# The last tile's four strided stores: issued by SyncE and ScalarE instead of SyncE and GpSimd

## The chip, the cores and the metric

The kernel runs on one core of a Trainium2 chip. A core has five engines with an instruction stream each: TensorE (PE, with its weight loads as PEld), VectorE (DVE), ScalarE (ACT), GpSimd (POOL) and SyncE (SP). Transfers between the core's memory and the chip's large memory are issued by an instruction on one of these streams and then run by themselves on 16 DMA engines; a semaphore tells when a transfer has landed. The metric is the device time of one execution, in microseconds, as the median of several runs.

## The reference

A sorting attention is followed by a Fourier mixing block. Four batches of 768 tokens with 8 heads of 64 go through the attention; its result, seen as 768 x 512 per batch, goes through a two-dimensional Fourier transform, a normalisation and a two-layer network:

```python
X = np.fft.fft(x, axis=1)
X = np.fft.fft(X, axis=2)
mixed = np.real(X).astype(np.float32)
u = x + mixed
mu = np.mean(u, axis=-1, keepdims=True)
var = np.mean((u - mu) ** 2, axis=-1, keepdims=True)
un = (u - mu) / np.sqrt(var + 1e-06)
ch = np.maximum(un @ w_ch1, 0.0) @ w_ch2
return (u + ch).astype(np.float32)
```

`x` is the attention's output; `w_ch1` is 512 x 2048 and `w_ch2` 2048 x 512. The output has 4 x 768 x 512 values of 32 bits.

## The kernel before

The host program builds one list of *steps* for all four batches. A step has a name, the engines that it may run on with a cost for each, a function that writes the instructions, the tiles that it reads and writes, and, for a DMA, the time of its transfer (`work`) and of its latency (`hop`). A planner (`Plan`, L187 to L379) keeps an estimate of when each engine is free (`free`), when the DMA queue of each issuing engine is free (`dma`) and when the eight semaphore lanes of each issuing engine are free (`lanes`). `run` (L334) takes, again and again, the step that could start earliest; `emit` (L269) writes it and moves the estimates. The planner's output is the order of the instructions on each engine. It is made on the host and costs no device time. Semaphore waits between the instructions are put in when the program is built, from what each one reads and writes.

The end of the program is the network of batch 3, second half (`mlp`, L1108). For 128 tokens at a time PE adds up 16 matmuls into one bank (L1150), VectorE adds the residual and writes a tile `outt` of 128 x 512 values (L1158), and `store` (L1163) sends it to `out`. In the Fourier part the tokens lie in another order than in the output. So 23 of the 24 tiles are written by an indirect DMA on GpSimd (L1173), which takes the row numbers from a table. The last tile, batch 3 tile 5, holds four groups of tokens that lie at a fixed stride in the output (32, 24, 24 and 48 rows), and `store` writes it with four direct DMAs at L1169. Before the change SyncE issues three of these and GpSimd the second one, of 24 rows. Every store into `out` waits for the indirect stores into `out` ahead of it, since the program cannot know that their rows differ.

After the last instruction all engines meet: SyncE waits for the semaphores of the transfers, each engine drains what it has under way (an instruction DRAIN), the engines exchange semaphores, and GpSimd clears them. The profile gives all of this the line L1393, where the host program leaves the kernel.

Of the kernel before, what the change touches and what calls it, by code (L numbers as in the profile page):

```python
# [17 lines left out]
S = 768  # L18
# [3 lines left out]
G = 6  # L22
# [102 lines left out]
class Buf:  # L125
    __slots__ = ("tag", "t", "left", "free_at")

    def __init__(self, tag):
        self.tag, self.t, self.left, self.free_at = tag, None, 0, 0.0
# [57 lines left out]
class Plan:  # L187
# [15 lines left out]
    def __init__(self, engines):  # L203
        self.engines, self.rings = engines, {}
        self.wrote, self.read = {}, {}
        self.todo = []
        self.free = dict.fromkeys(engines, 0.0)
        self.dma = {"S": 0.0, "G": 0.0}
        self.lanes = {"S": [0.0] * 8, "G": [0.0] * 8}
        self.pool = (0.0, 0.0)  # L210
        self.under_way = []
        self.began = self.half = False
# [6 lines left out]
    def step(self, name, b, on, fn, r=(), w=(), work=0, hop=0, lanes=1, bulk=False, need=None, prio=None,  # L219
             rel=0.0):  # L220
        s = Step()
        s.name, s.b, s.on, s.fn, s.work, s.hop, s.rel = name, b, on, fn, work, hop, rel
        s.lanes, s.bulk, s.port = lanes, bulk, name in self.PORT
        s.data, s.pre, s.succ, s.fin, s.by, s.extra = set(), set(), set(), None, None, []
        for key in r:
            if key in self.wrote:
                s.data.add(self.wrote[key])
        s.pre |= s.data
        for key in w:
            if key in self.wrote:  # L230
                s.pre.add(self.wrote[key])
            s.pre.update(self.read.get(key, ()))
        for key in r:
            self.read.setdefault(key, set()).add(s)
        for key in w:
            self.wrote[key] = s
            self.read[key] = set()
        s.pre.discard(s)
        s.use = list(dict.fromkeys(
            k if isinstance(k, Buf) else k[0] for k in list(r) + list(w)  # L240
            if isinstance(k, Buf) or isinstance(k, tuple) and isinstance(k[0], Buf)))
        for u in s.use:
            u.left += 1
        s.prio = need - 90e3 if need is not None else prio
        self.todo.append(s)
        return s
# [70 lines left out]
    def start(self, free, dma, lanes, landed):  # L317
        for s in self.wrote.values():
            if s in self.todo:
                continue  # L320
            s.fin = free["T"]
            if landed.get(s.name):
                s.fin = max(s.fin, landed[s.name].pop(0))
        self.half = False
        self.free = dict(free)
        self.dma = dict.fromkeys("SG", dma)
        self.lanes = lanes
        for r in self.rings.values():
            if isinstance(r, Ring):
                for h in r.held:  # L330
                    if h is not None:
                        h.free_at = free["T"]
# [50 lines left out]
def kernel(  # L383
# [27 lines left out]
    plan = Plan({"T": nc.tensor, "V": nc.vector, "A": nc.scalar, "G": nc.gpsimd, "S": nc.sync})  # L411
    step, Buf = plan.step, plan.buf
# [695 lines left out]
    def mlp(b, gr):  # L1108
# [32 lines left out]
        for t in range(3):  # L1141
            pC = Buf("bank")
            for f4 in range(4):
                if f4 == 0 and t < 2:
                    load_u(t + 1)

                def f(e, t=t, f4=f4, pC=pC):
                    ps = bank(pC, [128, DM])
                    for fc in range(4 * f4, 4 * f4 + 4):
                        nc.tensor.matmul(ps, hr[f4].t[:, fc % 4, 128 * t:128 * (t + 1)],  # L1150
                                         w2sb[:, fc, :], start=(fc == 0), stop=(fc == 15))
                pc = ("pc", b, {"T": 870}, f, [(hr[f4], j) for j in range(4)] + [("w2", f4)], [pC, "mlp"])
                if f4 < 3:
                    plan.chain(pc, prio=MLP)
                    continue
                o = Buf("outt")
                plan.chain(pc, prio=MLP)
                step("outt", b, {"V": 687}, lambda e, t=t, pC=pC, o=o: nc.vector.scalar_tensor_tensor(  # L1158
                    o.t, ur[t].t, RSC, bank(pC, [128, DM]), op0=ALU.mult, op1=ALU.add),
                    [pC, ur[t]], [o], prio=MLP - 1e8)  # L1160
                store(b, 3 * gr + t, o, MLP - 1e8)

    def store(b, q_, o, prio):  # L1163
        if (b, q_) == (B - 1, 5):
            for y, (r, n, k0, st) in enumerate((
                    (0, 32, 2 * BLK + 33, 2), (32, 24, 3 * BLK, 4),
                    (56, 24, 3 * BLK + 2, 4), (80, 48, 3 * BLK + 1, 2))):
                e_ = "G" if y == 1 else "S"
                step("store", b, {e_: 400}, lambda e, r=r, n=n, k0=k0, st=st: plan.engines[e].dma_start(  # L1169
                    out[b, k0:k0 + st * (n - 1) + 1:st], o.t[r:r + n]), r=[o], work=300, hop=1300, prio=prio)  # L1170
            return
        c = 6 * b + q_
        step("store", b, {"G": 1050}, lambda e: nc.gpsimd.indirect_dma_start(  # L1173
            out=out.rearrange("b s m -> (b s) m"),
            out_offset=bass.IndirectOffsetOnAxis(ap=idx[:, c:c + 1], axis=0),
            in_=o.t, in_offset=None), r=[o, "idx"], work=800, hop=1400, prio=prio)
# [87 lines left out]
    for half in range(2):  # L1264
        make_kron(0, half, pcol)
    step("pca", 0, {"A": 390}, lambda e: nc.scalar.activation(pca, pcol(), AF.Copy, scale=XSC / BLK),
         r=[pC, (kron[0], 1)], w=["pca"])
# [62 lines left out]
    for b in range(B):  # L1330
# [10 lines left out]
        for h in range(H):  # L1341
            n = H * b + h
# [55 lines left out]
```

## Time and profile before

| what | value |
|---|---|
| median of 3 runs | 316.94 us |
| the three runs | 312.82, 316.96, 316.94 us |
| span of the profiled execution, first to last instruction | 312.2 us |
| time of the profiled execution itself | not listed; the runs above lie 0.6 to 4.8 us over its span |
| granted TensorE clock, mean | 0.985 |
| busy: PE, DVE, ACT, POOL | 287.7, 218.6, 206.3, 137.8 us |
| DMA issued by SyncE's queue (hardware_dynamic) | 39560 packets, 28.68 MB |
| DMA issued by GpSimd's queue (software_dynamic) | 14800 packets, 16.57 MB |

The profile shows one execution. Times within it count from its first instruction. An engine's name with a q behind it (SPq, POOLq) stands for the engine's instruction sequencer: semaphore instructions, drains and the issuing of DMAs, which count as no busy time of the engine. A row of the timeline gives start, duration, engine, line, operation, and what is written from what; in square brackets stands the idle time ahead of it and what ended it. A row of the view of one line gives the operation, how many there are, their shortest, median and longest duration in ns, and the start of the first and of the last.

### The profile page before, as it was taken

How to read it: one execution, taken by the hardware profiler on the slowest of the kernel's cores; microseconds unless marked ns; L12 is line 12 of the kernel's file. 1: busy time of each engine (PE TensorE's matmuls, PEld its weight loads, DVE VectorE, ACT ScalarE, POOL GpSimd, SP SyncE). 2: the span in 40 equal slices, each digit the busy share in tenths (PEclk: the TensorE clock that was granted, in tenths of full speed). 3: DMA queues.
4: the chain of work that ended last, by engine and by line, in shares of the span. 5: the costliest groups of instructions: out<-in, count | busy, mean ns of one | idle time of the engine just before them, and what ended most of it. 6: DMA issues, size and time to landing. Idle time of an engine off the chain costs nothing.

```text
span 312.2 us, 7389 instructions
## 1 busy us (share of the span) xinstructions
PE 287.7 (92%) x2715; PEld 181.9 (58%) x2715; DVE 218.6 (70%) x489; ACT 206.3 (66%) x486; POOL 137.8 (44%) x206
## 2 busy tenths in 40 slices
PE   8879599999999798999998999999999999999990
PEld 5657577866765454555654767646556755645540
DVE  6779779998997888787579999997466764010010
ACT  6587587999884567998676759887715754704500
POOL 8634166957125899446444115462021763112020
PEclk9999979999999999999999999999999999999996
DMA  7975886999699776996997444569334337314021
GB/s 214 172 189 92 172 208 96 171 207 219 129 141 213 194 229 111 144 243 171 180 225 132 104 119 96 147 188 212 75 92 135 104 100 215 80 67 136 0 101 35
DMA packets 54396, 45.72 MB, mean 146 GB/s; under 512 B 23393, under 2 KB 46144, under 8 KB 54360
## 3 DMA queue, kind: packets, MB, share of 16 engines
q1 hardware_dynamic: 39560, 28.68, 36.0%
q0 software_dynamic: 14800, 16.57, 30.6%
q8 instruction: 21, 0.34, 0.5%
q14 instruction: 15, 0.12, 0.2%
HBM read 35.33 MB, written 12.58 MB: 153 GB/s over the span
## 4 chain that ended last, share of the span: by engine, by line
PE 59%; DVE 15%; ACT 8%; DMA 5%; issue 5%; POOL 4%; SPq 1%; POOLq 0%; DVEq 0%; ACTq 0%
PE bank L1129 21%; PE bank L1150 21%; DVE kz L484 3%; PE bank L913 3%; DMA v<-in_v_dram 2%; DMA eT<-es 2%; ACT kz L480 2%; PE bank L868 2%; POOL u L1032 1%; POOL u L1033 1%; PE bank L982 1%; PE bank L821 1%; DVE xr L875 1%; ACT un L1075 1%; SPq L690 1%
## 5 line engine op out<-in xcount | busy, mean ns | idle before, releaser
L1129 PE MATMUL bank<-unT,w1sb 128*128 128x384 f16 x512 | 90.8, 326 | 1.3 <-ACT hr L1135 1.3
L1150 PE MATMUL bank<-w2sb,hr 128*128 128x512 f16 x384 | 90.5, 379 | 0.6 <-DVE W L482 0.6
L1135 ACT ACTIVATE hr<-bank 128x384 f16<-128x384 f32 x128 | 60.4, 495 | 28.6 <-PE bank L1129 27.6
L1129 PEld LDWEIGHTS <-w1sb 128*128 128x128 f16 x512 | 48.3, 98 | 31.8 <-issue 2.0
L1173 POOL DMA_INDIRECT out_dram<-outt,idx_sb x23 | 23.1, 1005 | 81.9 <-DVE outt L1158 61.5
L1150 PEld LDWEIGHTS <-hr 128*128 128x128 f16 x384 | 35.9, 98 | 38.3 <-issue 0.8
L1158 DVE SCALAR_TENSOR_TENSOR outt<-ur,bank 128x512 f32<-128x512 f32 x24 | 16.4, 682 | 38.8 <-PE bank L1150 38.8
L826 ACT ACTIVATE sm<-bank,mns 96x96 f32<-96x96 f32 x128 | 32.6, 354 | 4.8 <-DVE mns L831 4.6
L1050 DVE BATCH_NORM_STATS2 st<-u 96x6 f32<-96x512 f32 (+1 forms) x32 | 21.9, 683 | 4.2 <-POOL u L1033 4.0
L875 DVE TENSOR_TENSOR xr<-bank,rz 96x512 f16<-96x512 f32 x32 | 22.0, 686 | 1.1
L1032 POOL TENSOR_TENSOR u<-u,P 96x257 f32<-96x257 f32 (+1 forms) x16 | 11.9, 743 | 22.8 <-DVE P L990 10.9
L524 POOL TENSOR_TENSOR v<-v 128x384 f32<-128x384 f32 x11 | 11.1, 1013 | 18.3 <-ACT v L478 18.2
L484 DVE TENSOR_SCALAR kz<-bank 64x768 f16<-64x768 f32 x16 | 15.2, 952 | 4.9 <-ACT kz L480 3.4
L478 ACT COPY u<-bank 96x512 f32<-96x512 f32 (+1 forms) x21 | 12.1, 586 | 9.0 <-PE bank L1009 6.5
L1075 ACT ACTIVATE un<-u,nm,rstd 96x512 f16<-96x512 f32 (+1 forms) x16 | 13.0, 819 | 6.9 <-DVE nm L1064 6.9
L913 PE MATMUL bank<-cso_sb,xs 96*128 96x384 f16 x64 | 13.4, 332 | 3.9 <-ACT sm L808 2.7
L478 ACT CAST W<-bank 128x384 f16<-128x384 f32 (+1 forms) x29 | 10.6, 402 | 8.6 <-PE bank L913 6.1
L682 DVE SCALAR_TENSOR_TENSOR vo<-a,bank 128x384 f16<-128x384 f16 x32 | 15.7, 542 | 0.0
L480 ACT ACTIVATE kz<-bank 64x768 f16<-64x768 f32 x16 | 12.7, 803 | 4.3 <-DVE kz L484 3.2
L831 DVE TENSOR_REDUCE mns<-bank 96x8 f32<-96x768 f32 x16 | 14.9, 943 | 0.7 <-PE bank L821 0.7
L892 DVE TENSOR_TENSOR xs<-xr 96x512 f16<-96x512 f16 x32 | 14.6, 469 | 0.7 <-PE bank L929 0.2
L808 ACT ACTIVATE sm<-bank 96x768 f32<-96x768 f32 x16 | 12.8, 800 | 3.5 <-PE bank L803 2.8
(149 smaller groups left out, 539.9 us busy)
## 6 DMA issues: line engine op xcount, KB each, us to landing
u_dram<-u SPq DMA_DIRECT2D x32, 192.0 KB
ur<-u_dram SPq DMA_DIRECT2D x24, 256.0 KB
v<-in_v_dram SPq DMA_DIRECT2D x11, 384.0 KB
vs<-vo SPq DMA_DIRECT2D x48, 65.0 KB
k<-in_k_dram POOLq DMA_DIRECT2D x15, 192.0 KB, 4.4
q<-in_q_dram POOLq DMA_DIRECT2D x15, 192.0 KB, 5.0
w1sb<-in_moe_w_ch_dram POOLq DMA_DIRECT2D x4, 512.0 KB, 6.9
w2sb<-in_moe_w_ch_dram POOLq DMA_DIRECT2D x4, 512.0 KB, 6.0
```

Of the source, the lines that this page charges most:

```text
L478: nc.scalar.copy(dst, src)
L480: nc.scalar.activation(dst, src, AF.Copy, scale=scale)
L484: nc.vector.tensor_scalar(dst, src, scale, None, op0=ALU.mult)
L826: nc.scalar.activation(sm.t[:, i], pair(pS, BLK)[:, y, i % 4], AF.Exp, bias=mn.t[:, i:i + 1], scale=-1.0)
L875: nc.vector.tensor_tensor(xr2[b % 2][0:BLK, :, D * h:D * (h + 1)].rearrange("p (t j) d -> p t j d", t=2), ps[:, :, :, 0:D], r[:, :, :, Non ...
L913: nc.tensor.matmul(ps, xs[b, hp, 1].t[:, j, :], cso[:, j, :], start=(j == 0), stop=(j == 3))
L1050: nc.vector.bn_stats(st.t[0:n], us[b, i, m].t[0:n])
L1129: nc.tensor.matmul(ps, w1sb[:, mc, 128 * fc:128 * fc + 128], unT[b, gr].t[:, mc, :], start=(mc == 0), stop=(mc == 3))
L1135: nc.scalar.activation(dst, bank(pH, [128, 384]), AF.Relu)
L1150: nc.tensor.matmul(ps, hr[f4].t[:, fc % 4, 128 * t:128 * (t + 1)], w2sb[:, fc, :], start=(fc == 0), stop=(fc == 15))
L1158: step("outt", b, {"V": 687}, lambda e, t=t, pC=pC, o=o: nc.vector.scalar_tensor_tensor(o.t, ur[t].t, RSC, bank(pC, [128, DM]), op0=ALU.mu ...
L1173: step("store", b, {"G": 1050}, lambda e: nc.gpsimd.indirect_dma_start(out=out.rearrange("b s m -> (b s) m"), out_offset=bass.IndirectOffs ...
```

## The change

The last tile's four stores are issued by SyncE and ScalarE in turn: SyncE issues the first (32 rows) and the third (24 rows), ScalarE the second (24 rows) and the fourth (48 rows). Rows, strides and sizes stay as they are. GpSimd issues none of the four; its last DMA is the indirect store of the tile before. Since ScalarE now issues DMAs, the planner gets a queue and eight lanes for it; they start as the others do.

```diff
@@ Plan.__init__
-        self.dma = {"S": 0.0, "G": 0.0}
-        self.lanes = {"S": [0.0] * 8, "G": [0.0] * 8}
+        self.dma = dict.fromkeys("SGA", 0.0)
+        self.lanes = {e: [0.0] * 8 for e in "SGA"}
@@ Plan.start
-        self.dma = dict.fromkeys("SG", dma)
-        self.lanes = lanes
+        self.dma = dict.fromkeys("SGA", dma)
+        self.lanes = dict(lanes, A=[free["A"]] * 8)
@@ store
             for y, (r, n, k0, st) in enumerate((
                     (0, 32, 2 * BLK + 33, 2), (32, 24, 3 * BLK, 4),
                     (56, 24, 3 * BLK + 2, 4), (80, 48, 3 * BLK + 1, 2))):
-                e_ = "G" if y == 1 else "S"
-                step("store", b, {e_: 400}, lambda e, r=r, n=n, k0=k0, st=st: plan.engines[e].dma_start(
+                step("store", b, {"SA"[y % 2]: 400}, lambda e, r=r, n=n, k0=k0, st=st: plan.engines[e].dma_start(
                     out[b, k0:k0 + st * (n - 1) + 1:st], o.t[r:r + n]), r=[o], work=300, hop=1300, prio=prio)
             return
```

## The prediction, made before the result was known

> **What bounds the kernel now.** I read the page's head first, then the chain that ended last, then the timeline of the last microseconds, then the instructions that the profile puts on the closing line of the program (L1393, where all engines meet). The page says where the bulk lies:
>
> ```profile
> span 312.2 us, 7389 instructions
> PE 287.7 (92%) x2715; PEld 181.9 (58%) x2715; DVE 218.6 (70%) x489; ACT 206.3 (66%) x486; POOL 137.8 (44%) x206
> ```
>
> PE holds 92% of the span, and the change touches none of its work. What can move is only what comes after the last matmul. The chain of waits from 302 us shows it, and behind it the timeline from 303.7 us (start, duration, engine, line, operation):
>
> ```profile
> 302.17 2.73 DMA out_dram<-outt,idx_sb
> 304.90 0.02 issue
> 304.93 0.02 POOLq L1169
> 304.94 0.55 issue
> 305.50 0.62 POOLq L1393
> ```
>
> ```profile
> 303.76 0.38 PE L1150 MATMUL bank<-w2sb,hr 128*128 128x512 f16 x1
> 304.23 0.69 DVE L1158 SCALAR_TENSOR_TENSOR outt<-ur,bank 128x512 f32<-128x512 f32 x1 [2.76 <-PE bank L1150]
> 305.07 1.47 SPq L1169 DMA_DIRECT2D out_dram<-outt  x3
> 305.52 0.59 POOL L1169 DMA_DIRECT2D out_dram<-outt  x1 [2.38 <-DVE outt L1158]
> ```
>
> PE ends at 303.76 + 0.38 = 304.14 us, VectorE writes the last tile until 304.92, SP issues three stores from 305.07 to 306.54, POOL one from 305.52 to 306.11. The span ends at 312.2. So 5.7 us follow in which no engine computes. The instructions of the closing line tell what fills them (first and last start in us, durations in ns; the first two rows are the answer for the stretch 305.4 to 311.2, the others that for 308 to 313):
>
> ```profile
> L1393 SPq EVENT_SEMAPHORE  x9: 28/28/28, 307.6 to 308.5; - x9
> L1393 SPq DRAIN  x2: 7/7/7, 308.6 to 308.6; - x2
> L1393 POOLq DRAIN  x1: 5923/5923/5923, 305.5 to 305.5; - x1
> ...
> L1393 POOLq EVENT_SEMAPHORE  x4: 17/17/17, 311.5 to 312.1; - x4
> L1393 POOLq DRAIN  x3: 46/103/5923, 305.5 to 311.9; - x3
> ```
>
> This is the row that decides the case. SP waits at the close for the landings (nine semaphore instructions, the last at 308.5) and reports at 308.6. POOL starts one DRAIN at 305.5, as it issues its store, and that DRAIN takes 5.92 us, to 305.5 + 5.92 = 311.42; only at 311.5 does POOL take up the semaphores by which the engines meet. SP has then waited for 311.42 - 308.6 = 2.8 us. **The end of the span is set by POOL's drain behind its own store**; 312.2 - 311.42 = 0.78 us of meeting and clearing follow. The other two drains of POOL, at 311.6 to 311.9, take 0.10 and 0.05 us, so a drain is not long in itself. The transfers do not fill that gap either (times of the stretch, its length, then busy us of PE, PEld, DVE, ACT and POOL, clock, DMA share, GB/s):
>
> ```profile
> 307.00:308.00 1.00, 0.00 (x0) 0.00 (x0) 0.00 (x0) 0.00 (x0) 0.00 (x0) 0.50 0.38 107
> 308.00:309.00 1.00, 0.00 (x0) 0.00 (x0) 0.00 (x0) 0.00 (x0) 0.00 (x0) 0.50 0.00 0
> 309.00:312.20 3.20, 0.00 (x0) 0.00 (x0) 0.00 (x0) 0.00 (x0) 0.00 (x0) 0.50 0.00 0
> ```
>
> **The change part by part.** *Before the last tile: nothing.* The planner's new row "A" starts, like those of S and G, from the value that `start` is given and is raised only by a step that issues a DMA on A. The maximum over the rows and the charges of S and G are then the same until the last four stores. I cost the program up to 304.92 at 0.
>
> *Removed: POOL's store.* Its wait (0.02), the issue gap (0.55), the 0.59 us of the DMA and the drain behind it go. POOL's last work is then the indirect store ahead of it:
>
> ```profile
> 302.17 0.97 POOL L1173 DMA_INDIRECT out_dram<-outt,idx_sb  x1 [2.91 <-DVE outt L1158]
> ...
> L1169 POOL DMA_DIRECT2D out_dram<-outt x1: 592/592/592, 305.5 to 305.5; - x1
> DMA to landing us min/median/max: 2.1/2.1/2.1
> ```
>
> POOL's drain can start some 3 us earlier. What it waits for is not written in any row, so I bound its end by the three points that it can be counted from. From its own start, which coincides with the start of the last DMA: 302.17 + 5.92 = 308.09. From the end of that DMA's instruction: 311.42 - 306.11 = 5.31 us behind it, so 302.17 + 0.97 + 5.31 = 308.45. From its landing: the store landed at 305.52 + 2.1 = 307.6, the drain ended 3.8 us later; the indirect store lands at 302.17 + 2.73 = 304.90, so 308.70. All three lie within 0.6 us. Below them stands the drain without any tail (0.05 to 0.10 us, the other two rows): POOL would then be done at 303.2 and decide nothing. I take 308.45, the middle.
>
> One rule bears on this row. The Trainium skill, GPSIMD Engine Reference, section "Instruction dispatch", says that the first call of freshly loaded code costs about 6 us (5.95 measured there) without an instruction of its own in the profile. The 5.92 us here agree in size, though no row shows a code load; by that rule the price is fixed and is paid from the point where POOL stops, which is the first of the three points, 308.09.
>
> *Moved: the stores.* SP issues the 32-row and the second 24-row store, ACT the first 24-row and the 48-row one. ACT has no work left that this could delay:
>
> ```profile
> 293.88 0.49 ACT L1135 ACTIVATE hr<-bank 128x384 f16<-128x384 f32 x1 [0.16 <-PE bank L1129]
> ...
> L1169 SPq DMA_DIRECT2D out_dram<-outt x2: 336/364/391, 305.1 to 305.5; - x2
> ...
> L1169 SPq DMA_DIRECT2D out_dram<-outt x1: 324/324/324, 306.2 to 306.2; - x1
> ...
> SPq L1169 <- DMA out_dram<-outt,idx_sb: 6.4, 2, 3.5
> ```
>
> ACT is idle from 294.4. The added wait is the one that SP has already (last row): all indirect stores into `out` must have landed, the last at 304.90, and the tile must be written, 304.92. Both come together, and nothing but ACT's share of the closing meeting is queued behind ACT's stores, so ACT can issue from 305.07 as SP does. An issue by ACT is nowhere in this trace; the nearest rows are SP's three, 0.32 to 0.39 us, and the step from SP's first to its third store is 306.2 - 305.07 = 1.13 us, of which the 24-row store alone takes from about 305.45 to 306.2, 0.76 us. If ACT works like SP and beside it, its 48-row store starts at 305.07 + 0.76 = 305.83, 0.37 earlier than the same store on SP now, and SP reports at 308.6 - 0.37 = 308.25. If ACT needs twice SP's price, or the two queue for one another, it starts at 305.07 + 2 x 0.76 = 306.59, and SP reports at 309.0. I take 308.6, near the middle: today's time. All four stores use the same rows of the tile and the same bytes; POOL's transfer of 48 KB now starts a little earlier and may push the others by the little that is inside these bounds.
>
> **The sum.** The meeting begins at the later of POOL (308.09 to 308.70) and SP (308.25 to 309.0): I take 308.6, against 311.42 now. With the 0.78 us behind it the span ends at 309.4, bounds 309.0 to 309.8: 2.8 us less (2.4 to 3.2). The median of the runs shown, 316.94, is 4.74 us above the profiled span and the lowest, 312.82, 0.62 above; the time of the profiled execution itself is not given. I take the same 2.8 us off the median: 314.1 us (313.7 to 314.5), 0.9% less. What a measurement can tell from no change here is about 2%, and the three runs shown differ by 1.3% among themselves.
>
> **The rivals.**
>
> *The drain follows the last transfer of any queue.* Then POOL waits for more than its own stores, and a drain started earlier ends no earlier. SP's waits put the last landing at 308.4 (its last two semaphore instructions stand at 308.4 and 308.5), 3.0 us ahead of the drain's end. The 48-row store lands between 0.37 us earlier and 0.4 later, and the time is 316.6 to 317.3. Against it: DMA share is 0 from 308 on while the drain goes on. The Trainium skill, "DMA: Bandwidth & Descriptors", section "Issuing engines are not separate DMA queues", speaks in the same direction: all queues run on the same 16 engines, and spreading DMAs saves issue time alone. By that rule the change is worth the 0.37 us of issue, on an engine that is not last, and the time is 316.9. Chance 0.12.
>
> *The drain's tail grows with what POOL's last DMA moves: slower.* The indirect store now stands last, and it is larger:
>
> ```profile
> DMA packets 80, 0.26 MB, mean 219 GB/s; under 512 B 16, under 2 KB 16, under 8 KB 80
> ...
> q0 software_dynamic: 32, 0.05, 31.9%
> ```
>
> (the indirect store's packets between 303.5 and 304.7 us, and those of POOL's direct store between 306.6 and 307.3.) With packets the tail of 5.31 us becomes 5.31 x 80/32 = 13.3 us, POOL is done at 303.14 + 13.3 = 316.4, the span ends at 317.2 and the time is 321.9; counted from the landing, 3.8 x 2.5 = 9.5, it is 319.9. It costs time from the point where the tail is over 311.42 - 303.14 = 8.28 us, 1.56 times today's. For it: one long drain, behind one kind of DMA, cannot show a fixed price. Against it: the drain outlasts its transfer by 3.8 us, so bytes alone do not explain it. Chance 0.08.
>
> *ACT's own queue of DMAs costs something outside the span or at its first issue,* which no row prices: ACT issues no DMA now. It eats the gain when it comes to 2.8 us; bounded by nothing and by the 4.74 us that lie around the span at the median, it gives 314.1 to 318.8, with 316.5 in the middle. Chance 0.10.
>
> *The runs fall low.* One of three runs was 4.1 us below the other two, whatever the reason. If most of the new runs fall so, the median is 312.82 - 2.8 = 310.0. Chance 0.20.
>
> **How the numbers follow.** The forecast has the remaining 0.50. The range takes in the low runs and the rival without gain, 309.5 to 317.3; outside are the longer tail and a part of the queue's price, and a stray below, together under 0.2. Faster by over 2% means below 310.6: the low runs, 0.20. Slower by over 2% means above 323.3: only a longer tail together with a price for the queue, 0.03. The rest, 0.77, is within 2%.
>
> **What would show it.** In the changed profile POOL's long DRAIN should start at about 302.2 and end between 308.1 and 308.7; the SP semaphores of the closing line should end at 308.2 to 309.0; the two ACT stores should start near 305.1 and 305.8 and take 0.3 to 0.6 us; the last VectorE tile should still end near 304.9. I am wrong if the drain still ends near 311.4 (any queue), if it is longer than 8 us (packets), or if ACT's stores start late. A gain far from 2.4 to 3.2 us in the span would mean that the drain counts from something else.

## The result and the profile after

With the change the median of 12 runs is 311.21 us, against 314.97 us of 12 runs of the kernel before: a ratio of 0.9885 with a 95% interval of 0.9846 to 0.9924, or 3.6 us less (2.4 to 4.9). The same kernel, timed once more in a later run beside the kernel before, gave 0.9919 (0.9885 to 0.9953). It is a gain, and it is under the 2% mark. The ratio leaves out the slower runs of both kernels, of which the profiled execution of the changed kernel is one (315.81 us, its longest, granted clock 0.970), so its middle is not compared with anything here; only its close is.

The timeline of the changed kernel from 306.5 us, in the columns known from before (here and below the rows of PE and PEld are left out):

```profile
306.94 0.97 POOL L1172 DMA_INDIRECT out_dram<-outt,idx_sb  x1 [2.94 <-DVE outt L1158]
308.97 0.69 DVE L1158 SCALAR_TENSOR_TENSOR outt<-ur,bank 128x512 f32<-128x512 f32 x1 [2.76 <-PE bank L1150]
309.93 1.04 SPq L1168 DMA_DIRECT2D out_dram<-outt  x2
309.93 0.99 ACTq L1168 DMA_DIRECT2D out_dram<-outt  x2
```

And its closing line, now L1392, with the line of the four stores, L1168:

```profile
L1392 SPq EVENT_SEMAPHORE  x11: 17/28/28, 311.0 to 314.0; - x11
L1392 POOLq EVENT_SEMAPHORE  x4: 17/17/17, 313.3 to 313.9; - x4
L1392 POOLq DRAIN  x3: 46/97/6417, 306.7 to 313.8; - x3
L1392 SPq DRAIN  x3: 7/7/7, 313.2 to 313.5; - x3
...
L1168 SPq DMA_DIRECT2D out_dram<-outt x2: 333/334/336, 309.9 to 310.6; - x2
L1168 ACTq DMA_DIRECT2D out_dram<-outt x2: 349/476/603, 309.9 to 310.6; - x2
```

The last VectorE tile ends at 308.97 + 0.69 = 309.66 and the span at 314.0: 4.4 us lie between, where there were 312.2 - 304.92 = 7.3. POOL's long DRAIN now starts at 306.7, ahead of the last indirect store, and ends at 306.7 + 6.42 = 313.1. SP reports at 313.2 to 313.3 and POOL takes up the meeting at 313.3. POOL's drain and SP's waits for the landings, which were 2.8 us apart, end together. ACT's two stores are there, at 0.60 and 0.35 us. Up to the last stores each engine runs the same instructions in the same order in both traces, so the planner's new row moved nothing else.

### The profile page after: what moved, and what is told of

Its sections match the earlier page's. It is cut to its first block, busy times and chain, and to the rows that moved or that the text cites. A ratio compares the mean times of both kernels' runs of the same rounds, so it can differ in the third digit from the quotient of the medians.

```text
span 314.0 us, 7394 instructions
## 1 busy us (share of the span) xinstructions
PE 291.1 (93%) x2715; PEld 184.6 (59%) x2715; DVE 217.8 (69%) x489; ACT 206.3 (66%) x486; POOL 137.1 (44%) x205
## 4 chain that ended last, share of the span: by engine, by line
PE 57%; DMA 16%; POOL 7%; DVE 6%; ACT 5%; issue 3%; SPq 3%; POOLq 0%; DVEq 0%; ACTq 0%
PE bank L1150 22%; PE bank L1129 21%; DMA vs<-vo 5%; DMA w2sb<-in_moe_w_ch_dram 4%; DMA unT<-in_q_dram 4%; PE bank L913 2%; DMA u_dram<-u 2%; PE bank L868 2%; SPq L690 2%; DVE kz L484 1%; PE bank L821 1%; POOL u L1033 1%; POOL kz L1226 1%; POOL u L1032 1%; ACT kz L480 1%
## 5 line engine op out<-in xcount | busy, mean ns | idle before, releaser
L1150 PE MATMUL bank<-w2sb,hr 128*128 128x512 f16 x384 | 91.6, 382 | 2.2 <-DMA w2sb<-in_moe_w_ch_dram 2.2
L787 DVE TENSOR_REDUCE mxs<-bank 96x8 f16<-96x768 f32 x16 | 14.7, 946 | 0.8 <-PE bank L784 0.7
L868 PEld LDWEIGHTS <-eT 97*128 97x128 f16 (+1 forms) x256 | 11.6, 102 | 5.9 <-DMA vs<-vo 2.1
```

The costliest lines, as they stand in the source:

```text
L868: nc.tensor.matmul(ps[0:wide(i).stop - BLK * i, i // 4, i % 4], et[0:97, wide(i)], vs[2 * (b % 2) + h // 4][:, i, (D + 1) * (h % 4):(D + 1 ...
```

## The experiments

**What was to be told apart.** The theory on record: the end is set by POOL's closing drain, which counts from the end of POOL's own last DMA, and the change gains by letting POOL stop one tile earlier. Rivals: the gain is in issuing the stores from two engines; the drain follows the last transfer of any queue; the drain grows with what the last DMA moves; and, formed after the result, that the drain itself is dear and it does not matter what stands ahead of it.

All kernels are read by one table. "Tail" is the time from the end of the last VectorE tile to the end of the span, "drain" the end of POOL's closing drain and "SP" the moment at which SP reports, both counted from the end of that tile, "behind POOL" the time from the end of POOL's last instruction to the end of the drain, all in us from each kernel's trace:

| kernel | drain | behind POOL | SP | tail |
|---|---|---|---|---|
| before | 6.5 | 5.3 | 3.7 | 7.3 |
| the change | 3.5 | 5.2 | 3.6 | 4.4 |
| e11, the change again | 3.5 | 5.2 | 3.4 | 4.3 |
| e1, all four on SP | 3.6 | 5.2 | 3.9 | 4.7 |
| e2, POOL keeps its store, ACT helps | 6.5 | 5.3 | 3.5 | 7.3 |
| e4, the change and a POOL copy | 5.5 | 5.2 | 3.4 | 6.3 |
| e5, before and a middle drain | 2.9 | 1.6 | 3.5 | 4.3 |
| e6, the change and a middle drain | 0.1 | 1.9 | 3.6 | 4.4 |
| e7, three engines and a middle drain | 3.1 | 1.8 | 3.6 | 4.4 |
| e8, the change, largest first | 3.5 | 5.2 | 3.3 | 4.2 |
| e9, before and an early drain | 4.2 | 3.1 | 3.4 | 5.0 |
| e10, largest first and a middle drain | 0.2 | 1.9 | 3.4 | 4.2 |

In each row the tail is the later of the two ends plus 0.8 us, to the rounding. Of e4, e5, e8 and e9 there is one execution each, so they are read by these times within the trace and not by their total.

**e1: POOL's store away, ACT not used.**

```diff
-                step("store", b, {"SA"[y % 2]: 400}, ...
+                step("store", b, {"S": 400}, ...
```

> All four stores of the last tile are issued by SP, none by POOL and none by ACT: the change without its ACT part. Measure: from the end of the last VectorE tile to the end of the span (7.3 us before, 4.4 us with the change). Theory (POOL's closing drain counts some 5.3 us from the end of POOL's own last DMA instruction, and the change gains by ending POOL's DMAs one tile earlier): POOL's drain ends 3.5 us behind the tile as with the change, SP's landings come some 0.8 us later than with the change because of four issues in a row, so 5.0 to 5.4 us, and a ratio to before near 0.993. Rival (the gain is in issuing the stores from two engines at once): 7.3 us or more, ratio 1.00 or above. Rival (the drain follows the last transfer of any queue): the drain ends 3 us behind the last landing, 8 us.

Measured: ratio 0.9935 (0.9887 to 0.9983), tail 4.7 us. The timeline and the closing line of this kernel:

```profile
300.31 0.97 POOL L1172 DMA_INDIRECT out_dram<-outt,idx_sb  x1 [3.05 <-DMA out_dram<-outt,idx_sb]
302.23 0.69 DVE L1158 SCALAR_TENSOR_TENSOR outt<-ur,bank 128x512 f32<-128x512 f32 x1 [2.77 <-PE bank L1150]
303.21 1.84 SPq L1168 DMA_DIRECT2D out_dram<-outt  x4
...
L1392 POOLq DRAIN  x3: 46/97/6418, 300.1 to 307.3; - x3
L1392 SPq DRAIN  x3: 7/7/7, 306.8 to 307.1; - x3
```

The tile ends at 302.92, the drain at 300.1 + 6.42 = 306.5 and SP reports at 306.8. Taking the store off POOL alone brings the tail from 7.3 down to 4.7, where the whole change brings it to 4.4. The rival of two engines is wrong: without ACT nearly all of the gain is there. The rival of any queue is wrong too: here the drain ends before SP has its last landing. The tail was expected at 5.0 to 5.4 and came at 4.7: SP's four issues took 1.84 us, and SP reported only 0.3 us later than with the change.

**e2: ACT helps, POOL keeps its store.**

```diff
-                step("store", b, {"SA"[y % 2]: 400}, ...
+                step("store", b, {"SGSA"[y]: 400}, ...
```

> POOL keeps its 24-row store, ACT takes the 48-row store from SP: the ACT part of the change alone. Theory of POOL's own drain: it starts with POOL's store and ends 5.2 to 5.3 us behind that store's end as before, so 7.3 us from the last tile to the end of the span, ratio 1.00. Rival (issuing from more engines gains): 4.4 to 6.9 us, ratio 0.99 to 0.997.

Measured: ratio 1.0044 (0.999 to 1.0098), tail 7.3 us:

```profile
304.26 0.69 DVE L1158 SCALAR_TENSOR_TENSOR outt<-ur,bank 128x512 f32<-128x512 f32 x1 [2.77 <-PE bank L1150]
305.54 0.59 POOL L1168 DMA_DIRECT2D out_dram<-outt  x1 [2.38 <-DVE outt L1158]
...
L1392 POOLq DRAIN  x3: 46/103/5920, 305.5 to 311.9; - x3
L1392 SPq DRAIN  x3: 7/7/7, 308.4 to 311.7; - x3
```

SP reports at 308.4 instead of 308.6 and waits for the same drain, to 305.5 + 5.92 = 311.4. ACT's part of the change alone is worth nothing.

**e4: what does the drain count from?**

```diff
+            step("touch", b, {"G": 60}, lambda e: nc.gpsimd.tensor_copy(landed[0:1], o.t[0:1, 0:1]), r=[o], prio=prio)
             return
```

> The changed kernel with one more POOL instruction: a copy of one value of the last tile into a scratch tile, which waits for the last tile and so ends some 0.3 us behind it. It asks what POOL's closing drain counts from. If from POOL's last DMA instruction (something that the DMA leaves behind): the drain's end stays 5.2 to 5.3 us behind the end of the indirect store, and the span ends 4.4 us behind the last tile as with the change. If from the last instruction of any kind (the drain itself is dear, as with code that must be loaded first): the drain ends 5.2 to 5.3 us behind the copy, and the span ends 6.3 us behind the last tile.

```profile
303.43 0.97 POOL L1173 DMA_INDIRECT out_dram<-outt,idx_sb  x1 [2.93 <-DVE outt L1158]
305.47 0.69 DVE L1158 SCALAR_TENSOR_TENSOR outt<-ur,bank 128x512 f32<-128x512 f32 x1 [2.77 <-PE bank L1150]
306.22 0.18 POOL L1170 CAST landed<-outt 1x1 f16<-1x1 f32 x1 [1.83 <-DVE outt L1158]
...
L1393 POOLq DRAIN  x3: 46/97/5443, 306.2 to 312.2; - x3
L1393 SPq DRAIN  x3: 7/7/7, 309.5 to 311.9; - x3
```

The copy ends at 306.40 and the drain at 306.2 + 5.44 = 311.6, 5.2 us behind the copy and 7.2 us behind the DMA. The tail is 6.3 us, and SP has waited 2 us. So the theory's "behind the DMA" falls: a copy of one value brings two thirds of the loss back. The DMA had landed at 303.43 + 2.7 = 306.1, before the copy ended, so the drain did not wait for it. The 5.2 us are the drain's own, and at the close they count from the end of POOL's last instruction, whether that is a direct DMA, an indirect one or this copy. What they are spent on is not shown.

**e5: is every drain so dear?** In the kernel before, one more drain three tiles ahead of the last, in a stretch in which POOL waits:

```diff
+            if c == 20:
+                nc.gpsimd.drain()
```

> The kernel before with one more POOL DRAIN, behind the indirect store three tiles ahead of the last. If only a first drain is dear (code that must be loaded once): the new drain takes 5.9 us, the closing one under 0.7 us, SP's landings set the end, and the span ends 4.5 us behind the last tile instead of 7.3. If every drain behind a DMA takes 5.2 to 5.3 us from that DMA's end: both drains do, and it stays at 7.3 us. If drains of POOL in the middle end at the landing, the new one takes about 3 us.

The timeline, the middle drain (L1180), the closing line and POOL's store:

```profile
283.09 0.97 POOL L1175 DMA_INDIRECT out_dram<-outt,idx_sb  x1 [2.64 <-DVE outt L1158]
302.38 0.69 DVE L1158 SCALAR_TENSOR_TENSOR outt<-ur,bank 128x512 f32<-128x512 f32 x1 [2.77 <-PE bank L1150]
303.73 0.59 POOL L1169 DMA_DIRECT2D out_dram<-outt  x1 [2.37 <-DMA out_dram<-outt,idx_sb]
...
L1180 POOLq DRAIN  x1: 6624/6624/6624, 282.9 to 282.9; - x1
...
L1398 POOLq DRAIN  x3: 51/103/2255, 303.7 to 307.1; - x3
L1398 SPq DRAIN  x3: 7/7/7, 306.5 to 306.9; - x3
...
DMA to landing us min/median/max: 2.1/2.1/2.1
```

The middle drain takes 6.62 us and ends 5.4 behind its DMA, in the shadow of POOL's idle time. (e6, e7 and e10 have it too. It ends 5.25 to 5.65 us behind its DMA in the four, but in each 2.5 to 2.6 us behind the landing, which takes 3.7 to 4.1 us there and 2.7 at the close. There a later landing goes with a later end.) The closing one then takes 2.26 us: it ends at 303.7 + 2.26 = 306.0, some 0.2 us behind the landing at 303.73 + 2.1 = 305.8. The tail is 4.3 us with POOL still issuing its store: **what the change takes off the tail, one drain in an idle place takes off too.** Behind a drain that ended 14 us earlier, the closing one ends just after the landing.

**e6: the change and the middle drain** (both edits together).

> The changed kernel with a DRAIN of POOL behind the indirect store three tiles ahead of the last, where POOL is idle. If a drain that has run shortly before is cheap, POOL's closing drain ends with the landing of its last indirect store, within 0.3 us of the last VectorE tile, and not 3.5 us behind it; then SP's waits for the landings alone set the end, 4.3 to 4.4 us behind the last tile, as with the change (4.37): ratio to before as for the change, 0.985 to 0.993. If the cheap drain of the earlier run was a matter of the direct store being POOL's last, the drain stays at 3.5 us behind the tile.

```profile
304.26 0.69 DVE L1158 SCALAR_TENSOR_TENSOR outt<-ur,bank 128x512 f32<-128x512 f32 x1 [2.77 <-PE bank L1150]
...
L1397 POOLq DRAIN  x3: 46/97/3077, 302.0 to 309.1; - x3
L1397 SPq DRAIN  x3: 7/7/7, 308.5 to 308.8; - x3
```

POOL is done at 302.0 + 3.08 = 305.1, and SP at 308.5 sets the end; ratio 0.9893 (0.9849 to 0.9938). The tail stays where it was, 4.4, so behind the change nothing more is to be had from the drain alone: the landings end as late (in the change's two profiles once after the drain and once 0.1 us before it).

**e8, e7, e10: can the landings come earlier?** e8 lets SP issue 48 rows and then 24, ACT 32 and then 24:

```diff
-                    (0, 32, 2 * BLK + 33, 2), (32, 24, 3 * BLK, 4),
-                    (56, 24, 3 * BLK + 2, 4), (80, 48, 3 * BLK + 1, 2))):
+                    (80, 48, 3 * BLK + 1, 2), (0, 32, 2 * BLK + 33, 2),
+                    (32, 24, 3 * BLK, 4), (56, 24, 3 * BLK + 2, 4))):
```

> The changed kernel with its stores in another order: SP 48 rows then 24, ACT 32 rows then 24. Theory: POOL's drain ends 3.5 us behind the last tile whatever SP does, so the span ends 4.2 to 4.4 us behind it, no earlier than 0.15 us ahead of the change (4.37), even if SP's landings come 0.3 us earlier. Rival (the landings alone set the end): 4.0 to 4.1 us.

SP reports 3.3 us behind the tile, the drain ends at 3.5, the tail is 4.2 us, as the theory had it. e7 has the middle drain and this order with POOL back, `{"SAGS"[y]: 400}`:

> Mid drain on POOL, and the four stores over three engines with the largest first: SP 48 rows, then the second 24; ACT 32 rows; POOL the first 24. With the cheap drain, POOL's store costs no tail: POOL is done about 2.9 us behind the last tile, SP 3.0 to 3.4, and the span ends 3.8 to 4.2 us behind the last tile (4.37 with the change, 7.3 before): ratio 0.985 to 0.992. If the drain is dear whenever a direct store stands last, the end is at 7.3 us as before.

Its tail is 4.4 us and not 3.8 to 4.2; the ratio is 0.9955 (0.9915 to 0.9995). The cheap drain is there (3.1 us behind the tile), but the stores from three engines land no earlier, and SP reports at 3.6. e10 is e8 with the middle drain:

> The changed kernel with both the DRAIN of POOL three tiles ahead of the last and the order of e8 (SP 48 rows then 24, ACT 32 rows then 24). POOL should be done 0.2 us behind the last tile, SP 3.3 us as in e8, so the span ends 4.0 to 4.15 us behind the last tile, 0.1 to 0.2 us under e8 (4.25) and 0.3 under the change (4.37). Against the change that is 0.1%, below what the times can tell; the ratio to before should be 0.985 to 0.991. If POOL's drain plays no part in e8, it stays at 4.2 to 4.3.

Its tail is 4.2 us and not 4.0 to 4.15, with POOL done at 0.2 and SP at 3.4; ratio 0.9876 (0.9806 to 0.9946). SP reported 0.1 us later than in e8, so taking the drain away bought nothing there. With e8's it is the shortest tail measured, but 0.2 us under the change is less than the times can tell, and SP's report itself came at 3.6 and at 3.4 in two profiles of the changed kernel.

**e11: the change once more.**

> The change itself once more, beside the kernel before on the same chip as the run above, for a profile that is less disturbed in its middle. The tail from the last VectorE tile to the end of the span should be 4.3 to 4.5 us again, with POOL's drain ending 5.2 us behind the end of the indirect store, and the ratio to before 0.985 to 0.992.

Tail 4.3 us, the drain 5.2 us behind POOL, ratio 0.9919: as expected.

**e9: how long does a drain keep?** The drain of e5 behind the first indirect store instead (`c == 0`):

> The kernel before with the additional DRAIN of POOL behind its first indirect store, at about 103 us, with some 60 POOL operations of other kinds between it and the close. If only the first drain behind the start is dear, the closing one is cheap (2.3 us) and the span ends 4.3 us behind the last tile. If a drain becomes dear again when POOL has done other work in between, both take 5.2 us from the end of what stands ahead of them, and it stays at 7.3 us. The drain in the middle can also delay the work there; only the close is to be compared.

```profile
104.60 1.09 POOL L1175 DMA_INDIRECT out_dram<-outt,idx_sb  x1 [0.17 <-issue]
109.39 0.72 POOL L1032 TENSOR_TENSOR u<-u,P 96x257 f32<-96x257 f32 x1 [3.70 <-issue]
...
L1180 POOLq DRAIN  x1: 6991/6991/6991, 102.3 to 102.3; - x1
...
L1398 POOLq DRAIN  x3: 46/103/3707, 308.8 to 313.0; - x3
L1398 SPq DRAIN  x3: 7/7/7, 311.6 to 312.8; - x3
```

Neither expectation holds. The early drain ends at 102.3 + 6.99 = 109.3 and holds POOL up for 3.7 us behind its DMA (104.60 + 1.09 = 105.69 to 109.39), and the closing drain, 200 us later, ends 3.1 us behind POOL's store: less than 5.3, more than 1.6. The tail is 5.0.

**A reading that no run tests.** The price of a drain may grow with what POOL has issued since its last one. The first row is POOL's first drain of the program, in the kernel before; the others are the packets of POOL's queue in e9 up to 109.3 us and from there on (number, MB, share of the DMA engines):

```profile
L1382 POOLq DRAIN  x1: 192/192/192, 0.3 to 0.3; - x1
...
q0 software_dynamic: 9200, 8.00, 51.2%
...
q0 software_dynamic: 5600, 8.57, 18.6%
```

With no packet behind it that first drain took 0.19 us. With 160 to 192 packets since the last drain the closing one ended 1.6 to 1.9 us behind POOL's last instruction (e5, e6, e7, e10), with 5600 it was 3.1, with 9200 it was 3.6, and with 14608 to 14800 it was 5.2 to 5.65. The order fits in every trace, e4's among them, and the time since the last drain does not give it: 102 us stand before the 3.6 and 200 us before the 3.1. But no run changes the packets alone, so this is a guess to be tested and not a cause.

## Why the prediction was right, and where it was not

*That the drain sets the end, and that 2.8 us go:* right. The tail fell from 7.3 to 4.4 us, 2.9 us; e1 and e2 show that POOL's store carried it and ACT's part did not. The sum ended on SP's report, 3.7 us behind the tile, with POOL 0.15 us ahead of it; measured were 3.4 to 3.6 for SP and 3.5 for POOL. The measured 0.9885 stands beside the 0.991 that the forecast comes to (314.1 / 316.94), inside the interval.

*What the drain counts from:* the value taken, 5.31 us from the end of POOL's last DMA, came out at 5.2, so the sum was good. The other two points were off by some 0.3 us each: from the start of the DMA the drain ended 313.1 - 306.94 = 6.2 us later and not 5.92, and from the landing at 306.94 + 2.7 = 309.6 it ended 3.5 us later and not 3.8. But all three points tied the end to POOL's last DMA, and e4 shows that it need not be one: the drain was as long behind a copy, with that DMA landed. Counting from the DMA held because a DMA happened to be POOL's last instruction in both kernels, and 5.31 us from one direct DMA held for an indirect one without a row that said so. That much was luck.

*The rule weighed there,* in the Trainium skill, GPSIMD Engine Reference, section "Instruction dispatch": a first call of freshly loaded code costs about 6 us. The prediction put this at 308.09, which counts from the start of the DMA; POOL stops at its end, 303.14, and 5.92 us from there is 309.06. Measured from that end were 5.2 us. A dear drain and a cheap one soon after (e4, e5) would fit such a rule, but POOL's first drain of the program took 0.19 us, so the dear one is not the first; that code is loaded is shown by no row, and e9's 3.1 us fit neither a first call nor a later one. What makes a drain dear stays open.

*The stores:* SP was taken to report at today's 3.7 us behind the tile, and did at 3.4 to 3.6. The two engines do queue for one another: SP's second store started 0.70 us behind its first (309.93 and about 310.63), as in every kernel here in which ACT issues, where the kernel before and e1 had 0.38, and ACT's first issue took 0.60 us. The 0.76 us that the prediction gave a 24-row store are no fixed price: in e1 SP went on 0.76 us after the first of them and 0.37 us after the second. So ACT gives 0.3 to 0.5 us against four stores on SP (e1: 3.9), and no more. That is the size of the issue time, as the Trainium skill has it in "DMA: Bandwidth & Descriptors", section "Issuing engines are not separate DMA queues". That the change would be worth no more than this, as the rival took from that rule, did not hold here, because of the drain.

*The rivals:* the last transfer of any queue is refuted by e1, and by e6, where POOL is done 3.4 us before SP reports; the tail that grows with size by the change itself, 5.2 us behind 80 packets against 5.3 behind 32; a price of ACT's queue outside the span shows nowhere, the time lying 1.7 to 1.9 us over the span in every timed run, with ACT's queue or without.

*The absolute time* is the term that was mis-sized. The forecast took the median of three runs, 316.94, and put 4.74 us around the profiled span. With 1.8 us around it, that execution took some 314.0 us by estimate, and the median of 12 runs is 314.97. The predicted 314.1 is 2.9 us above the measured 311.21: about 2.0 from that median, the rest from the gain, 3.8 between the medians instead of 2.8. So 311.21 lies outside the 313.7 to 314.5 that the sum allowed, and the range held only because it reached down for the low runs: that rival, with 310.0, came nearer to the time than the forecast did.

## What to carry to other kernels

Read the closing line of a program like any other stage: which engine reports last, and since when the others have waited. GpSimd's closing drain cost 5.2 us here behind what GpSimd did last, a DMA or a copy, so let it stop early, or let it drain once in an idle place shortly before the end. When the closing is shared by two waits, only the later one pays, and after the first cut here they ended within 0.2 us of one another.

## What was not expected of the hardware

A drain on GpSimd ended 5.2 to 5.65 us behind the instruction ahead of it, but only 1.6 to 1.9 us, and 0.2 us or less behind the landing, when another drain had ended 10 to 14 us before, and 3.1 us with another 200 us before. It cost as much behind a copy of one value as behind an indirect store of 256 KB. And the profile's row of a drain starts ahead of the instruction in front of it (306.7 against 306.94 with the change, 102.3 against 104.60 in e9), so that its duration alone (5.92, 6.42, 5.44 us) misleads; at the close its end, counted from the end of that instruction, was the steady number.
